# Block 2 computed with tokens on partitions one batch earlier, in a fused linear-attention and MLP kernel

## The chip, the cores and the metric

One core of one Trainium2 chip runs one program. The metric is the device time of one execution in microseconds (us), taken several times. The kernel before takes 304.78 us (median of 4 runs, 304.0 to 305.3, beside the changed kernel). TensorE is called PE, VectorE DVE, ScalarE ACT, GpSimd POOL and SyncE SP, as the profile does.

## The reference

Eight batches of eight heads with 576 tokens of 64 channels go through a linear attention with a norm. The 4608 x 512 result goes through two matrix products with a leaky rectifier between them.

```
kv  = einsum('bhsd,bhse->bhde', k, v)                   # 64 x 64 per head
out = einsum('bhsd,bhde->bhse', q, kv)
rms = sqrt(mean(out * out, -1) + 1e-6)
x   = (out / rms * g_norm) -> (4608, 512)               # 8 heads x 64 side by side
h   = x @ w_in                                          # 512 x 2048
g   = maximum(h, 0) + alpha * minimum(h, 0)
y   = g @ w_out                                         # 2048 x 512, float32
```

## The kernel before

The 4608 tokens are worked in nine windows of 512. In each, 16 groups of the hidden dimension pass through `m1` (four matmuls `h_ps`, then ACT `m_sb` and DVE `gt`), and `y_mm` multiplies the `gt` of the window before by `w_out`. Beside this stream, PE prepares the attention of the coming windows ("block w"), in one of two ways:

- *Channels on partitions* (batches below `NB_PE`): PE transposes q (`qt_ps`), multiplies (`ot_ps`), and sums squares with another matmul (`ssq_ps`); ACT and DVE make the norm.
- *Tokens on partitions* (batches from `NB_PE` on): one DMA transposes q (`qtm`). PE multiplies one tile of 128 tokens at a time (`otm_ps`), ACT, DVE and POOL make the norm along the free axis, and small DMA transposes bring the tile back into `xm`. PE does less here, since it transposes nothing and sums no squares.

```
NB_PE = 3
def load(b, nm, h0=0, h1=H):             # two DMAs, issued on GpSimd
    nc.gpsimd.dma_start(...); nc.gpsimd.dma_start(...)
def regroup_batch(b):                    # copies into the matmul layout
    for nm in ("k", "q"): regroup(b, nm, eng=nc.gpsimd)
...
def transpose_q(b):                      # issued on SyncE
    qtms[b] = attn_p.tile([P, NT * NPAIR, P], FP16, name="qtm")
    nc.sync.dma_start_transpose(out=qtms[b][:], in_=...bufs[b % NBUF]["q"]...)
...
# after the y matmuls of window 0 (about 52 us):
regroup_batch(2)
steps = window_steps(2)                  # block 2, channels on partitions
for g in range(NF):
    if g == 3:
        load_batch(3)
        regroup_batch(3)
    m1_group(1, g)
    ...                                  # one step of block 2, a y matmul, another step
    if g == NF - 4: nc.sync.dma_start(out=g_all[:], in_=g_norm[:].partition_broadcast(P))
    if g == NF - 3: transpose_q(3)
```

The opening is a chain without that stream: batch 0 is loaded in halves and goes through q transposes, kv, `ot`, `ssq` and norms. `keep_warm(n)` puts n matmuls on constant data between them, to keep PE busy.

## Time and profile before

| | before |
|---|---|
| median of 4 runs | 304.78 us |
| span of the profiled run (305.35 us) | 303.6 us |
| PE busy | 285.6 us (94%) |
| PE waits in block 2 (about 54 to 100 us) | 3.2 us |
| stretch at half clock | 22.4 to 29.2 us |
| steady stream of window 0 starts, ends | 23.83, 38.12 us |
| first group of window 1 starts | 54.43 us |

PE is nearly full, so one reads where it is not, and where its clock is halved. The prediction shows those lines. One more view is the timeline of POOL (columns: start, length, engine, line, operation, output and input, count, and in brackets the idle time before it with what ended that).

```profile
50.21 2.32 POOL L106 COPY qsb<-qst 128x2560 f16<-128x2560 f16 x1 [0.63 <-DMA qst<-in_q_dram]
52.47 0.68 POOL L96 DMA_DIRECT2D kst<-in_k_dram  x1
```

POOL regroups q of batch 2 and issues the loads of batch 3 directly after it. The issue stands behind the regroup on the same engine: in this order the loads are not issued before the data of batch 2 has come in and been copied.

### The profile page before, as it was taken

To read this page: it belongs to the slowest core of one execution; us is meant where nothing else is said; L and a number is where in the kernel's file an instruction comes from. 1 tells how busy PE (TensorE), PEld (TensorE's weight loads), DVE (VectorE), ACT (ScalarE), POOL (GpSimd) and SP (SyncE) were. 2 spreads that over 40 slices of the span, in tenths; PEclk is the share of its full clock that TensorE was granted. 3 is DMA by queue.
4 is the path that set the end of the run, shared out by engine and by line. 5 is a ranking of instruction groups with operands and counts; after the bars stand their busy time and mean duration, and the time that the engine had idled before them with its cause. 6 is when DMAs were issued, how large, how long until landed. Compare 5 with 4: busy or idle time off the path is not lost.

```text
span 303.6 us, 4204 instructions
## 1 busy us (share of the span) xinstructions
PE 285.6 (94%) x1526; PEld 136.6 (45%) x1526; DVE 163.1 (54%) x249; ACT 156.5 (52%) x298; POOL 96.8 (32%) x105
## 2 busy tenths in 40 slices
PE   5769999988999899999999999999999999999993
PEld 2423454453554455445544544455444444444441
DVE  4545853557665548544964585459546844344200
ACT  1364617749586338434844574458437544443320
POOL 9923306730018504660566056404101300000000
PEclk9995999999999999999999999999999999999999
DMA  7999999993118983995289839954311411112233
GB/s 95 189 206 200 203 203 163 147 195 89 35 35 96 193 189 28 147 213 136 56 122 214 148 69 149 185 119 70 79 35 37 95 35 35 37 40 55 45 71 69
DMA packets 61156, 34.33 MB, mean 113 GB/s; under 512 B 27840, under 2 KB 56528, under 8 KB 61136
## 3 DMA queue, kind: packets, MB, share of 16 engines
q0 software_dynamic: 29664, 18.35, 43.7%
q1 hardware_dynamic: 31472, 15.71, 24.5%
q8 instruction: 12, 0.20, 0.3%
q14 instruction: 8, 0.07, 0.1%
HBM read 36.74 MB, written 9.44 MB: 152 GB/s over the span
## 4 chain that ended last, share of the span: by engine, by line
PE 83%; ACT 4%; POOL 4%; DVE 3%; issue 2%; DMA 2%; POOLq 0%; ACTq 0%; DVEq 0%
PE h_ps L421 38%; PE y_ps L443 35%; PE kv_ps L231 3%; DMA qst<-in_q_dram 2%; PE otm_ps L339 2%; ACT m_sb L428 2%; ACT rstd L274 1%; POOL rg L363 1%; DVE gt L430 1%; PE qt_ps L210 1%; PE ssq_ps L272 1%; PE yc L443 1%; PE yb L443 1%; PE ya L443 1%; POOL qst L96 1%
## 5 line engine op out<-in xcount | busy, mean ns | idle before, releaser
L430 DVE SCALAR_TENSOR_TENSOR gt<-m_sb,beta_sb,h_ps 128x512 f16<-128x512 f32 x144 | 106.7, 744 | 81.9 <-ACT m_sb L428 81.1
L443 PE MATMUL y_ps<-w_out_sb,gt 128*128 128x512 f16 x528 | 134.8, 379 | 0.0
L428 ACT ACTIVATE m_sb<-h_ps 128x512 f32<-128x512 f32 x144 | 85.8, 597 | 92.4 <-PE h_ps L421 92.3
L421 PE MATMUL h_ps<-xm,w_in_sb 128*128 128x512 f16 x384 | 98.5, 379 | 0.0
L421 PEld LDWEIGHTS <-w_in_sb 128*128 128x128 f16 x576 | 55.7, 99 | 68.7 <-issue 10.0
L443 PEld LDWEIGHTS <-gt 128*128 128x128 f16 x576 | 55.9, 98 | 65.9 <-issue 2.2
L363 POOL TENSOR_TENSOR rg<-ss,g_all 128x512 f32<-128x512 f32 (+1 forms) x25 | 26.1, 1045 | 93.0 <-ACT ss L361 93.0
L421 PE MATMUL h_ps<-xt,w_in_sb 128*128 128x512 f16 x192 | 50.4, 397 | 3.4 <-DVE gt L430 1.9
L450 ACT COPY y_sb<-y_ps 128x512 f32<-128x512 f32 x33 | 19.2, 583 | 17.5 <-PE y_ps L443 17.4
L351 DVE TENSOR_REDUCE ss<-sqm_sb 128x8 f32<-128x512 f32 (+1 forms) x25 | 17.1, 683 | 8.3 <-ACT sqm_sb L345 8.2
L106 POOL COPY ksb<-kst 128x2560 f16<-128x2560 f16 x6 | 13.9, 2318 | 20.9 <-DMA kst<-in_k_dram 20.9
L372 DVE TENSOR_TENSOR xrow<-otm_ps,rg 128x512 f16<-128x512 f32 (+1 forms) x25 | 17.0, 681 | 6.4 <-POOL rg L363 6.4
L345 ACT ACTIVATE sqm_sb<-otm_ps 128x512 f32<-128x512 f32 (+1 forms) x25 | 14.8, 593 | 6.9 <-PE otm_ps L339 6.9
L106 POOL COPY qsb<-qst 128x2560 f16<-128x2560 f16 x6 | 13.9, 2323 | 12.0 <-DMA qst<-in_q_dram 12.0
L283 DVE SCALAR_TENSOR_TENSOR xt<-ot_ps,g2col,rstd 128x512 f16<-128x512 f32 x12 | 8.9, 749 | 12.0 <-ACT rstd L277 12.0
L262 ACT ACTIVATE sq_sb<-ot_ps 128x512 f16<-128x512 f32 x12 | 6.9, 589 | 15.7 <-PE ot_ps L256 15.7
L231 PE MATMUL kv_ps<-vst,ksb 128*128 128x128 f16 x160 | 10.4, 219 | 1.9 <-DVE qt_sb L219 1.3
L231 PEld LDWEIGHTS <-ksb 128*128 128x128 f16 x160 | 9.5, 98 | 5.5 <-DVE ksb L106 2.4
L274 ACT ACTIVATE rstd<-ssq_ps,eps_t 128x512 f32<-128x512 f32 x12 | 8.2, 684 | 4.5 <-PE ssq_ps L272 4.5
L339 PEld LDWEIGHTS <-qtm 128*128 128x128 f16 x100 | 7.7, 98 | 5.9
L339 PE MATMUL otm_ps<-kv_sb,qtm 128*128 128x128 f16 x100 | 9.7, 219 | 0.0
L195 PE MATMUL warm_ps<-warm,mask 128*128 128x512 f16 x15 | 6.0, 555 | 3.1 <-DVE eps_t L138 3.1
(56 smaller groups left out, 135.0 us busy)
## 6 DMA issues: line engine op xcount, KB each, us to landing
out_dram<-y_sb SPq DMA_DIRECT2D x72, 128.0 KB, 2.4
kst<-in_k_dram POOLq DMA_DIRECT2D x7, 320.0 KB, 5.4
qst<-in_q_dram POOLq DMA_DIRECT2D x7, 320.0 KB, 8.3
vst<-in_v_dram POOLq DMA_DIRECT2D x7, 320.0 KB, 10.8
w_in_sb<-in_moe_w_in_dram POOLq DMA_DIRECT2D x4, 512.0 KB, 10.1
w_out_sb<-in_moe_w_out_dram POOLq DMA_DIRECT2D x4, 512.0 KB, 16.0
kst<-in_k_dram POOLq DMA_DIRECT2D x7, 256.0 KB, 7.1
qst<-in_q_dram POOLq DMA_DIRECT2D x7, 256.0 KB, 9.7
```

Source lines behind the costliest of these rows:

```text
L106: (eng or nc.vector).tensor_copy(out=bufs[b % NBUF][nm][:, :, h0:h1, :].rearrange("p t h d -> p h t d"), in_=stages[b % NBUF][nm][:, h0:h1],)
L231: nc.tensor.matmul(out=kv_ps[:, j - j0, :], lhsT=ks(t), rhs=vs(t), start=(t == 0), stop=(t == NT - 1),)
L339: nc.tensor.matmul(out=ot_ps[:, 2 * j : 2 * j + 2, :], lhsT=qtms[b][:, t * NPAIR + j, :], rhs=kvs[b, j], start=True, stop=True,)
L345: nc.scalar.activation(out=sq[0:n], in_=ot_ps[0:n], func=AF.Square)
L351: nc.vector.tensor_reduce(out=ss[0:n], in_=sq[0:n], op=ALU.add, axis=mybir.AxisListType.X,)
L363: nc.gpsimd.tensor_tensor(out=rg[0:n], in0=ss[0:n].unsqueeze(2).to_broadcast([n, H, D]), in1=g_all[0:n].unsqueeze(1).to_broadcast([n, H, D ...
L372: nc.vector.tensor_mul(out=x[0:n], in0=ot_ps[0:n], in1=rg[0:n])
L421: nc.tensor.matmul(out=h_ps[:], lhsT=w_in_blk(c, g), rhs=xt_of(w, c), start=(c == 0), stop=(c == NC - 1),)
L428: nc.scalar.activation(out=m_sb[:], in_=h_ps[:], func=AF.Relu, scale=-1.0)
L430: nc.vector.scalar_tensor_tensor(out=gt[:], in0=m_sb[:], scalar=beta_sb[:, g : g + 1], in1=h_ps[:], op0=ALU.mult, op1=ALU.add,)
L443: nc.tensor.matmul(out=y[:], lhsT=gts[w, g][:, a * P : (a + 1) * P], rhs=w_out_blk(g), start=(g == 0), stop=(g == NF - 1),)
L450: nc.scalar.copy(out=y_sb[:], in_=y[:])
```

## The change

It computes block 2 with tokens on partitions too (`NB_PE` 2), since that takes less PE time. The q of batch 2 is regrouped on DVE (it comes first now) and transposed by DMA during window 0. The opening gets more keep-warm matmuls and other buffers, so that its clock does not dip. The norm weights `g_all`, wanted earlier now, are spread over the partitions by a matmul instead of a late DMA. The loads of batch 3 stand, in the source, before window 1, and k of batch 2 is regrouped on DVE there; batch 3 is regrouped later in window 1 than before (group 9 instead of 3).

```diff
-    NB_PE = 3
+    NB_PE = 2
 ...
-        for nm in ("k", "q", "v"):        # load_batch; regroup_batch likewise
+        for nm in ("q", "k", "v"):
 ...                                       # opening (cut: the other keep_warm lines)
-    keep_warm(3)
+    keep_warm(4)
     step_kv(0, 0, 2)
+    keep_warm(2)
 ...
+    diag = const_p.tile([P, D], FP32, name="diag")
+    nc.vector.tensor_scalar(
+        out=diag[0:D], in0=ident[0:D, 0:D], scalar1=g2col[0:D], scalar2=None, op0=ALU.mult,
+    )
+    g_ps = ps_y.tile([P, D], FP32, name="g_ps", tag="y")
+    nc.tensor.matmul(out=g_ps[:], lhsT=ones32[0:D], rhs=diag[0:D], start=True, stop=True)
+    nc.vector.tensor_copy(out=g_all[:], in_=g_ps[:])
 ...
-    step_ot(0, 2)
+    step_ot(0, 2, (ps_o, "o2"))
 ...                                       # in the y matmuls of window 0
+        if g == 9:
+            regroup(2, "q")                # on DVE
+            transpose_q(2)
+        if g == 13:
+            load_batch(3)
+            regroup(2, "k")                # on DVE
 ...
-    regroup_batch(2)
-    steps = window_steps(2)                # (cut: the whole loop of window 1 as above)
-    for w in range(2, NW):
+    for w in range(1, NW):                 # window 1 joins the common loop
```

More of the change, by code (lines that the diff above doesn't have):

```diff
@@ L111, in load_batch @@
     def load_batch(b):
-        for nm in ("k", "q", "v"):
+        for nm in ("q", "k", "v"):
             load(b, nm)
     def regroup_batch(b):
-        for nm in ("k", "q"):
+        for nm in ("q", "k"):
             regroup(b, nm, eng=nc.gpsimd)
@@ L134 @@
     nc.vector.tensor_copy(out=mask16[:], in_=mask32[:])
+    ones32 = const_p.tile([P, P], FP32, name="ones32")
+    nc.vector.memset(ones32[:], 1.0)
     warm16 = const_p.tile([P, W], FP16, name="warm16")
@@ L148 @@
     nc.sync.dma_start(out=alpha_row[:], in_=moe_alpha[:].rearrange("(g p) -> g p", p=P))
-    g_all = const_p.tile([P, D], FP32, name="g_all")
     WQ = 4
@@ L189, with keep_warm @@
         load_w_out(i)
-    def keep_warm(n):
-        ps = ps_s.tile([P, W], FP32, name="warm_ps", tag="s")
+    def keep_warm(n, pool=(ps_s, "s")):
+        ps = pool[0].tile([P, W], FP32, name="warm_ps", tag=pool[1])
         for i in range(n):
@@ L267, in step_ssq, with ssq_mm @@
         norm(w, j)
-    def ssq_mm(w, j):
+    def ssq_mm(w, j, pool=(ps_o, "o2")):
         ot_ps, sq = ots.pop((w, j))
-        ssq_ps = ps_o.tile([P, W], FP32, name="ssq_ps", tag="o2")
+        ssq_ps = pool[0].tile([P, W], FP32, name="ssq_ps", tag=pool[1])
         nc.tensor.matmul(out=ssq_ps[:], lhsT=mask16[:], rhs=sq[:], start=True, stop=True)
@@ L483 @@
     )
+    diag = const_p.tile([P, D], FP32, name="diag")
[3 more added lines that the diff above has]
+    g_ps = ps_y.tile([P, D], FP32, name="g_ps", tag="y")
+    nc.tensor.matmul(
+        out=g_ps[:], lhsT=ones32[0:D], rhs=diag[0:D], start=True, stop=True,
+    )
+    g_all = const_p.tile([P, D], FP32, name="g_all")
+    nc.vector.tensor_copy(out=g_all[:], in_=g_ps[:])
     regroup(0, "k", HH, H)
     ssq_mm(0, 0)
+    keep_warm(3)
     ssq_mm(0, 1)
+    norm(0, 0)
+    keep_warm(3)
     step_kv(0, 2, 4)
-    norm(0, 0)
     norm(0, 1)
-    step_ot(0, 2)
+    step_ot(0, 2, (ps_o, "o2"))
     step_ot(0, 3, (ps_y, "y"))
@@ L493 @@
     first = [ps_h.tile([P, W], FP32, name="h_ps", tag="h") for g in range(3)]
-    for g in range(3):
+    m1_mm(first[0], 0, 0, (0, 1))
+    ssq_mm(0, 2, (ps_s, "s"))
+    for g in (1, 2):
         m1_mm(first[g], 0, g, (0, 1))
-    step_ssq(0, 2)
-    keep_warm(2)
-    step_ssq(0, 3)
+    ssq_mm(0, 3, (ps_o, "o0"))
+    keep_warm(6, (ps_o, "o1"))
+    norm(0, 2)
+    norm(0, 3)
     for g in range(3):
         m1_mm(first[g], 0, g, (2,))
+    keep_warm(2, (ps_o, "o1"))
     for g in range(3):
@@ L524 @@
                 steps.pop(0)()
+        if g == 9:
[4 more added lines that the diff above has]
+            regroup(2, "k")
     for a in range(AHEAD):
         y_out(ys[a], 0, a)
-    regroup_batch(2)
-    steps = window_steps(2)
-    n = len(steps)
-    y = ps_y.tile([P, W], FP32, name="y_ps", tag="y")
-    for g in range(NF):
-        if g == 3:
-            load_batch(3)
-            regroup_batch(3)
-        m1_group(1, g)
-        if g > 3 and steps:
-            steps.pop(0)()
-        y_mm(y, 0, AHEAD, g)
-        if g > 3 and steps:
-            steps.pop(0)()
-        if g == NF - 4:
-            nc.sync.dma_start(out=g_all[:], in_=g_norm[:].partition_broadcast(P))
-        if g == NF - 3:
-            transpose_q(3)
-    y_out(y, 0, AHEAD)
     LOAD_G = 6
-    for w in range(2, NW):
+    for w in range(1, NW):
         steps = phase_steps(w + 1)
         for g in range(NF):
-            if g == LOAD_G and w + 2 < B:
+            if g == LOAD_G and 3 < w + 2 < B:
                 load_batch(w + 2)
             a, part = divmod(g, TPW)
-            if part == 0:
-                pool, tag = ((ps_y, "y"), (ps_s, "s"))[a % 2]
-                y = pool.tile([P, W], FP32, name="y_ps", tag=tag)
+            parts = range(part * TPW, (part + 1) * TPW)
+            if w == 1:
+                a, parts = AHEAD, [g]
             begin, mid, end = steps.pop(0) if steps else ([], [], [])
@@ L567 @@
                 f()
-            for gg in range(part * TPW, (part + 1) * TPW):
+            if parts[0] == 0:
+                pool, tag = ((ps_y, "y"), (ps_s, "s"))[a % 2 if w > 1 else 0]
+                y = pool.tile([P, W], FP32, name="y_ps", tag=tag)
+            for gg in parts:
                 y_mm(y, w - 1, a, gg)
-            if part == TPW - 1:
+            if parts[-1] == NF - 1:
                 y_out(y, w - 1, a)
```

## The prediction

> **What bounds the kernel now.** I read the page first, then the windows, the PE timeline and the DMA views. On the page, TensorE is busy in almost every slice, and the chain that ended last runs mostly through its matmuls:
>
> ```profile
> PE   5769999988999899999999999999999999999993
> PEclk9995999999999999999999999999999999999999
> DMA  7999999993118983995289839954311411112233
> ...
> PE 83%; ACT 4%; POOL 4%; DVE 3%; issue 2%; DMA 2%; POOLq 0%; ACTq 0%; DVEq 0%
> ```
>
> From about 75 us on there is little to win: 512-column matmuls start every 0.216 us (four `h_ps` pieces of the chain last 0.86 us) and the stores at the end remain. Time can come only from the opening, from block 2 (52 to 99 us), and from fewer matmuls. The PEclk row has a dip in the fourth slice, with PE rows under 9 before it. The windows show why (columns: stretch, length, PE, PEld, DVE, ACT, POOL busy, granted clock, DMA share, GB/s):
>
> ```profile
> 16.00:19.00 3.00, 2.69 (x11) 0.99 (x11) 0.88 (x2) 1.52 (x3) 0.76 (x1) 1.00 1.24 205
> 19.00:22.40 3.40, 1.59 (x6) 0.57 (x6) 1.50 (x2) 2.09 (x4) 0.94 (x2) 1.00 1.25 207
> 22.40:25.80 3.40, 2.65 (x7) 0.84 (x6) 2.06 (x3) 1.64 (x4) 1.19 (x2) 0.50 1.33 200
> 25.80:29.20 3.40, 3.40 (x9) 1.18 (x8) 1.49 (x2) 1.18 (x3) 1.49 (x2) 0.50 1.41 201
> 29.20:32.60 3.40, 3.40 (x17) 1.56 (x16) 2.36 (x4) 2.33 (x4) 1.38 (x2) 1.00 1.28 202
> ```
>
> A stretch with PE 47% busy is followed by two at clock 0.50: 9 matmuls in 3.4 us instead of 17. The DMA queue, too, is full from the start (about 200 GB/s) until 51 us. PE's idle time in block 2, from its timeline:
>
> ```profile
> 61.45 1.28 PE L231 MATMUL kv_ps<-vst,ksb 128*128 128x128 f16 x20 [1.34 <-DVE qt_sb L219]
> ...
> 71.15 0.38 PE L272 MATMUL ssq_ps<-sq_sb,mask 128*128 128x512 f16 x1 [0.55 <-ACT sq_sb L262]
> ...
> 99.42 1.02 PE L421 MATMUL h_ps<-xt,w_in_sb 128*128 128x512 f16 x4 [0.87 <-DVE gt L430]
> ```
>
> With two smaller ones (0.18, 0.25) that is 3.2 us. The last is GpSimd's: six load issues (92.8 to 96.9) stood before a norm product.
>
> **What the Trainium skill says.** "TensorE: Matmul & The Clock Gate", Part 1: the clock is gated to half when PE was not busy enough in a free-running window of 3413 ns, and freed after a busy one. The trace agrees: half clock from 22.4 to 29.2, two such windows. "DMA: Bandwidth & Descriptors", section "SWDGE vs HWDGE vs iDMA": loads issued from GpSimd and transfers issued from SyncE feed different queues of the same 16 engines, which take turns between them. The trace agrees. In 103 to 105 us, with both waiting, nearly as many packets of one as of the other passed (columns: packets, MB, share of 16 engines):
>
> ```profile
> q0 software_dynamic: 448, 0.28, 93.6%
> q1 hardware_dynamic: 409, 0.10, 38.4%
> ```
>
> Same page, "Latency and other measured facts": a DMA transpose reaches 261 GB/s. Alone it does here: 271 GB/s in 108 to 110 us.
>
> **The change, part by part.**
>
> *Opening.* Keep-warm matmuls go from 15 to 30, and two norms and two buffers move. (a) The clock: the slow window gets eight more matmuls (6 + 2, some 1.7 us at 0.216), so it goes from 47% to near 90% busy, and the clock should hold. From 23.83, when the steady stream starts, to 29.20 it ran at half: 5.37 / 2 = **2.7 us** won. (b) The cost: `g_ps` stands before the first `ssq` on PE and waits for beta and then the diagonal on DVE. Beta starts at 13.19 and takes 0.17, the diagonal about as long, and the fp32 matmul as long as `alpha_ps` (0.23). The first `ssq` moves from 12.79 to about 14.0. Against this, `ot` 2 no longer waits for the norm at 16.27 (its bank is another). Working the ACT chain through with the timeline's durations (Ln 0.69, Exp 0.63, square 0.58, norm 0.75), the steady stream starts at about 24.1, so **0.3 us** is lost. Net **-2.4**. The weights keep ahead: the last `w_in` lands at 24.7, `w_out` at 33.9, 39.1, 41.6 and 44.5 against needs of 35.7, 41.4, 45 and 48.7.
>
> *Block 2 on PE.* Removed: 20 transposes x 0.056, four `ot` (0.22 each), four `ssq` (0.22), the old tail of 4 x 0.083 and 2 x 0.163: 3.5 us. Added: five tiles x 4 x 0.056, a tail of 4 x 0.056 and one `ssq`: 1.55 us. Net **-1.95**.
>
> *Waits of block 2.* The wait for `qt_sb` has no counterpart, and the three norm products now stand ahead of the regroups and loads: **-3.2**.
>
> *g by a matmul.* The broadcast DMA (6.7 us to landing) is gone; it was hidden before. **0** besides (b).
>
> *New wait 1: kv of batch 2.* It was at 61.45, and moves to just after the first group of window 1: y starts at 35.7 instead of 38.1, so that group starts at about 52.0 and ends at 52.9. v of batch 2 lands at 53.1, k's regroup ends at about 53.3: **+0.5**.
>
> *New wait 2: the transposed q of batch 2.* q lands at 47.1; the regroup on DVE follows a norm and ends at about 48.7. Then comes a DMA transpose of 655 KB in 2560 packets of 256 B. Before, such transposes ran on an empty queue. The DMA view of 92 to 108 us has one, with its time from issue to landing in us:
>
> ```profile
> qtm<-qsb SPq DMA_TRANSPOSE x1, 4.5
> ```
>
> The small transposes of `xm` (91 to 101 us), at most 512 packets each:
>
> ```profile
> DMA to landing us min/median/max: 4.0/6.3/8.0
> ```
>
> 8.0 is one of 512 under load: some 4 us until its first packet, then about 200 packets per us. At 48.7 the queue is now not empty: before, batch 3's loads were issued at 52.5, because GpSimd's own regroup of batch 2 held them. Nothing on GpSimd holds them now; each waits only for the load eight before it (w_out's third, landed at 41.6, for the first), wherever the source puts the call. So 3072 packets of batch 3 pass together with the transpose. My estimate: 48.7 + 4 + 2560 / 215 + 0.6 = 65.2. The first tile wants it on PE at 52.0 + three groups of 1.08 + kv 1.1 + wait 0.5 + tail 0.4, about 57.3. **+8**. An idle PE also loses its clock: one or two windows at half, of which I count **+1.5**.
>
> Sum: -2.4 - 1.95 - 3.2 + 0.5 + 8 + 1.5 = +2.5, which is 307.
>
> **The rivals.**
> *A: the transpose comes in time.* For it: I found no transpose of this size under load, and the share of turns is read from small ones; q is loaded first and regrouped on DVE, which shows a design for just this. Then another engine binds window 1 for a while: one y matmul per group makes a group 1.08 us long on PE, plus 0.22 for a tile, while DVE has gt, the reduction and xrow (0.74 + 0.68 + 0.68, some 0.2 less back to back). Three tiles cost about 1.5 us. Sum: -7.55 + 0.5 + 1.5 = -5.5, **299**.
> *B: the clock dips again* because the windows lie elsewhere in other runs: +2.7 on either.
> *C: a middle course*: the engines serve pairs faster (280 per us, as the separate rates of 370 and 1130 would allow), the landing is 62, the wait 4.5 us and the clock costs less: **303 to 304**.
> Against the main line speaks only that its size is carried from 512 packets to 2560; for it, that every issue and landing up to 48 us follows from the same queue as before.
>
> **Range and chances.** I weigh the main line (307) at a little over half, A (299) at a third, and C between: the point is 304.5, and 299 to 309 should hold it 8 times in 10. Two per cent are 298.5 and 310.7. Faster needs A with less than 1.5 us of tile waits: 0.13. Slower needs the full wait with two slow windows and more: 0.05. Within: 0.82.
>
> **What would show each step.** Clock 1.0 from 9 us to at least 57; the steady stream starting at about 24 and y at 35.7. Keep-warm count 30. kv of batch 2 starting at 53.3 after a wait for `vst` or `ksb`. PE's `otm_ps` waiting for the DMA of `qtm`, with that DMA 13 to 17 us from issue to landing and the loads of batch 3 issued before 51 us; then half clock. No PE idle before the last groups of window 2. The prediction is wrong if that DMA lands in under 9 us, or if the opening's dip stays.

## The result, and the profile after

The changed kernel takes 308.78 us (median of 4 runs, 308.4 to 309.8). The ratio to the kernel before is 1.014, with a 95% interval of 1.011 to 1.017: within 2%, but clearly slower. Ratios here are the mean time of one kernel's fast runs over that of the other's fast runs of the same rounds, so they are not quite the ratio of the medians. The profiled spans are 306.7 us after and 303.6 us before.

The page of the kernel after, with the rows of busy tenths and the chain that ended last:

```profile
PE   5698999549999999999999999999999999999993
PEclk9999999959999999999999999999999999999998
DMA  7999999992524993897169919943311411112233
...
PE 84%; DMA 7%; DVE 2%; POOL 2%; ACT 2%; issue 1%; POOLq 0%; ACTq 0%
```

The dip of the clock in the fourth slice is gone, and a new one stands in the ninth, where PE (slices 8 and 9) is at 5 and 4. The chain now holds 7% of DMA where it held 2%. The windows of the kernel after (columns as in the prediction) give both places:

```profile
19.00:22.40 3.40, 3.36 (x17) 1.40 (x16) 0.77 (x2) 3.29 (x6) 0.69 (x1) 1.00 1.25 207
22.40:25.80 3.40, 2.36 (x11) 0.94 (x10) 2.30 (x4) 1.57 (x3) 1.14 (x2) 1.00 1.30 205
...
58.50:62.00 3.50, 0.00 (x0) 0.00 (x0) 1.40 (x2) 0.68 (x2) 0.00 (x0) 1.00 1.33 186
62.00:65.50 3.50, 0.00 (x0) 0.00 (x0) 0.00 (x0) 0.00 (x0) 0.00 (x0) 0.52 1.30 212
65.50:69.00 3.50, 3.26 (x14) 1.74 (x15) 0.96 (x2) 1.47 (x4) 0.00 (x0) 0.51 0.57 187
69.00:72.00 3.00, 3.00 (x18) 1.49 (x17) 2.84 (x5) 2.57 (x7) 2.06 (x2) 1.00 0.00 0
```

In the opening PE does 17 matmuls where it did 6, and the clock stays at 1.00. From 58.5 to 65.5 PE does nothing at all. The clock falls in the middle of that, and comes back at 69. PE's timeline names what it waited for:

```profile
14.43 0.43 PE L492 MATMUL g_ps<-diag,ones 64*128 64x64 f32 x2 [0.98 <-DVE diag L488]
...
25.03 2.32 PE L422 MATMUL h_ps<-xt,w_in_sb 128*128 128x512 f16 x10 [1.03 <-DVE gt L431]
...
54.23 1.29 PE L232 MATMUL kv_ps<-vst,ksb 128*128 128x128 f16 x20 [0.36 <-DVE ksb L106]
...
65.74 0.61 PE L340 MATMUL otm_ps<-kv_sb,qtm 128*128 128x128 f16 x4 [7.41 <-DMA qtm<-qsb]
```

The last line is the loss: the first tile of batch 2 waits 7.41 us for its transposed q. The chain of waits says when that DMA was issued and how long it took (columns: start, length, what):

```profile
49.60 16.09 DMA qtm<-qsb
```

The prediction showed a transfer of the same size at 4.5 us (that of batch 4, issued at 106.5, with the last loads gone by 108). The DMA view of 54 to 64 us shows the company (columns: packets, MB, share of 16 engines), and POOL's timeline where it comes from:

```profile
q0 software_dynamic: 2279, 1.27, 87.9%
q1 hardware_dynamic: 2281, 0.58, 43.7%
```

```profile
42.45 0.68 POOL L96 DMA_DIRECT2D qst<-in_q_dram  x1 [2.12 <-DVE qt_sb L220]
...
51.16 0.69 POOL L96 DMA_DIRECT2D vst<-in_v_dram  x1 [2.78 <-PE ya L444]
```

The loads of batch 3 are issued from 42.45 us on; before, the first was issued at 52.47. No regroup on POOL holds them any more. In ten microseconds the engines passed 2279 packets of loads and 2281 of the transpose, 228 per us each: as many of one as of the other.

The balance of the two profiled runs, by PE's timeline, in us (after minus before; the fewer matmuls are the prediction's count):

| term | difference |
|---|---|
| first group of window 1 starts at 52.83 instead of 54.43 | -1.60 |
| wait for `qtm` | +7.41 |
| wait for k of batch 2 (`ksb`) | +0.36 |
| PE's work at half clock, 65.74 to 68.94, half of it lost | +1.60 |
| a wait for `gt` at 75 us that was not there | +0.59 |
| waits of block 2 that went away | -3.19 |
| fewer matmuls | -1.95 |
| sum | +3.22 |
| spans: 306.7 - 303.6 | +3.1 |

So the change does what it was meant to do, and loses more to one transfer. The measured times differ by about 4.2 us (0.0139 x 304.8), more than the profiles: the profiled run of before took 305.35 us, a little over the four timed beside it.

### The profile page after: what moved, and what is told of

It reads as the page before. It is cut to its first block, busy times and chain, and to the rows that moved or that the text cites. A ratio compares the mean times of both kernels' runs of the same rounds, so it can differ in the third digit from the quotient of the medians.

```text
span 306.7 us, 4237 instructions
## 1 busy us (share of the span) xinstructions
PE 284.5 (93%) x1530; PEld 136.7 (45%) x1530; DVE 166.9 (54%) x255; ACT 153.2 (50%) x298; POOL 97.3 (32%) x108
## 4 chain that ended last, share of the span: by engine, by line
PE 84%; DMA 7%; DVE 2%; POOL 2%; ACT 2%; issue 1%; POOLq 0%; ACTq 0%
PE h_ps L422 38%; PE y_ps L444 37%; DMA qtm<-qsb 5%; PE kv_ps L232 3%; PE otm_ps L340 2%; DMA vst<-in_v_dram 2%; PE warm_ps L196 1%; ACT m_sb L429 1%; PE ssq_ps L273 1%; DVE gt L431 1%; PE ya L444 1%; PE yc L444 1%; PE yb L444 1%; PE qt_ps L211 1%; PE ot_ps L257 1%
## 5 line engine op out<-in xcount | busy, mean ns | idle before, releaser
L422 PE MATMUL h_ps<-xm,w_in_sb 128*128 128x512 f16 x448 | 115.0, 379 | 0.0
L364 POOL TENSOR_TENSOR rg<-ss,g_all 128x512 f32<-128x512 f32 (+1 forms) x30 | 31.3, 1042 | 99.5 <-ACT ss L362 98.7
L422 PE MATMUL h_ps<-xt,w_in_sb 128*128 128x512 f16 x128 | 32.2, 388 | 1.9 <-DVE gt L431 1.9
L352 DVE TENSOR_REDUCE ss<-sqm_sb 128x8 f32<-128x512 f32 (+1 forms) x30 | 20.5, 683 | 16.1 <-ACT sqm_sb L346 16.0
L346 ACT ACTIVATE sqm_sb<-otm_ps 128x512 f32<-128x512 f32 (+1 forms) x30 | 17.8, 592 | 15.8 <-PE otm_ps L340 15.7
L373 DVE TENSOR_TENSOR xrow<-otm_ps,rg 128x512 f16<-128x512 f32 (+1 forms) x30 | 20.5, 682 | 3.6 <-POOL rg L364 3.6
L340 PE MATMUL otm_ps<-kv_sb,qtm 128*128 128x128 f16 x120 | 12.1, 225 | 7.4 <-DMA qtm<-qsb 7.4
L196 PE MATMUL warm_ps<-warm,mask 128*128 128x512 f16 x30 | 9.7, 461 | 3.8 <-DVE eps_t L140 3.3
L284 DVE SCALAR_TENSOR_TENSOR xt<-ot_ps,g2col,rstd 128x512 f16<-128x512 f32 x8 | 6.0, 750 | 9.2 <-ACT rstd L278 9.2
L359 ACT ACTIVATE ss<-ss,eps_t 128x8 f32<-128x8 f32 (+1 forms) x30 | 9.0, 300 | 2.9 <-DVE ss L352 2.9
```

Of the source, the lines that this page charges most:

```text
L340: nc.tensor.matmul(out=ot_ps[:, 2 * j : 2 * j + 2, :], lhsT=qtms[b][:, t * NPAIR + j, :], rhs=kvs[b, j], start=True, stop=True,)
L346: nc.scalar.activation(out=sq[0:n], in_=ot_ps[0:n], func=AF.Square)
L352: nc.vector.tensor_reduce(out=ss[0:n], in_=sq[0:n], op=ALU.add, axis=mybir.AxisListType.X,)
L364: nc.gpsimd.tensor_tensor(out=rg[0:n], in0=ss[0:n].unsqueeze(2).to_broadcast([n, H, D]), in1=g_all[0:n].unsqueeze(1).to_broadcast([n, H, D ...
L373: nc.vector.tensor_mul(out=x[0:n], in0=ot_ps[0:n], in1=rg[0:n])
L422: nc.tensor.matmul(out=h_ps[:], lhsT=w_in_blk(c, g), rhs=xt_of(w, c), start=(c == 0), stop=(c == NC - 1),)
```

## The experiments

The theory: the transpose is late because the loads of batch 3 share the DMA engines with it, packet for packet. The main rival: a transpose of this size, issued there, is late anyway, and only a smaller or an earlier one would help. A second question is what the opening gained and what the `g_ps` matmul cost in it. Each call ran on one chip with its own runs of the kernel before. Three calls took eleven runs; their medians of before were 304.23, 305.24 and 305.34 us.

**e1_hold3: the transpose alone.** A copy of four columns of `qtm` on POOL, ahead of the loads of batch 3, holds them until the transpose has landed. Nothing else is changed.

```diff
         if g == 13:
+            held = const_p.tile([P, 4], FP16, name="held")
+            nc.gpsimd.tensor_copy(out=held[:], in_=qtms[2][:, 0, 0:4])
             load_batch(3)
```

> The changed kernel, but GpSimd issues batch 3's loads only after the transposed q of batch 2 has landed (it first copies four of its columns). Theory T (the transpose took 16 us because its packets take turns with those of batch 3's loads): the transpose lands before 58 us, under 9 us after its issue, PE waits for it less than 0.5 us instead of 7.4, the clock stays at 1.0, and some 1 us of tile waits on DVE appears instead of the slow clock: about 300.5 us, 8 less than the changed kernel. Rival U (a transpose of 2560 packets takes this long at that place anyway, or batch 2's own loads hold it up): it still takes over 12 us and the time stays above 306. Possible new wait: kv of batch 3 at the start of window 2, since its v lands some 7 us later.

Measured: 301.12 us (300.91 to 301.43), ratio 0.990 (0.986 to 0.995). Answers of the trace on `qtm`, of POOL's timeline, and of the list of PE's waits (total, times, longest):

```profile
DMA to landing us min/median/max: 7.4/7.4/7.4
```

```profile
56.89 0.19 POOL L549 COPY held<-qtm 128x4 f16<-128x4 f16 x1 [16.80 <-DMA qtm<-qsb]
57.38 0.68 POOL L96 DMA_DIRECT2D qst<-in_q_dram  x1 [0.30 <-issue]
```

```profile
PE otm_ps L340 <- DVE xm L314: 1.2, 1, 1.2
```

The transfer takes 7.4 us instead of 16.1, PE does not wait for it, and the clock stays at 1.00 from the opening on. Nothing about the transpose itself was changed, so the rival falls: the late landing is the company. By the ratios the kernel gains 0.0235 x 304.5 = 7.2 us over the kernel after (the run of before at 308.0 is slow and left out of the ratios). The trace accounts for it: 7.41 + 1.60 won, 1.20 lost to a new wait for a PSUM bank that the tile shares with the norm of the tail, about 0.5 to one more wait for `gt` and 0.24 to a longer one for kv: 7.1.

**e2_split5 and e3_split2: leave the loads, cut the transpose.** The transpose is one DMA of five tiles; PE needs only the first to go on. e2 issues one DMA per tile, e3 one of three tiles and one of two. The loads of batch 3 stay early.

```diff
-        nc.sync.dma_start_transpose(out=qtms[b][:], ...)
+        for t0, t1 in ([(t, t + 1) for t in range(NT)] if b == 2 else [(0, NT)]):   # e3: [(0, 3), (3, NT)]
+            nc.sync.dma_start_transpose(
+                out=qtms[b][:, t0 * NPAIR : t1 * NPAIR, :], in_=...["q"][:, t0:t1]...)
```

> The changed kernel, with batch 2's q transposed in five DMAs, one tile (512 packets) each, loads as in the changed kernel. T: the first lands about 57 us (4 us to its first packet, 512 packets at about 225 per us, 0.6 to land), the others 2.3 us apart, so that PE waits under 1 us in total for the first three and the time is about 301 us. U (the transpose is slow as such): the sum over five issues is no quicker, the first tile still waits over 5 us, 306 or more.

> The same in two DMAs, the first with the three tiles that window 2 needs (1536 packets), the second with two. T: the first lands at about 49.6 + 3.6 + 1536 / 230 + 0.6 = 60.5 us, so PE waits some 2.2 us (7.4 in the changed kernel, with 2560 packets); the clock holds; about 302.5 us. A wait that does not follow the number of packets would be against T.

e2 measured 300.91 us (300.34 to 301.23), ratio 0.990 (0.984 to 0.996). Its five parts landed at 56.2, 58.6, 61.1, 63.4 and 65.5 us: one every 2.3 us, each ahead of its tile. So the last q still comes at 65.5, as in the kernel after, and costs nothing. The times to landing, and the first tile in PE's timeline:

```profile
DMA to landing us min/median/max: 7.3/9.5/10.9
```

```profile
58.88 0.38 PE L342 MATMUL otm_ps<-kv_sb,qtm 128*128 128x128 f16 x4 [1.20 <-DVE xm L314]
```

What is left there is the wait for the PSUM bank, as in e1. e3 had one run: 303.81 us, its state unknown. Its first part landed at 60.84 against an expected 60.5, and PE waited less than half as long. The expectation had the clock hold and the time at 302.5; both were missed: the clock was slow from 61.64 to 65.06, one window instead of two. Its waits of PE:

```profile
PE otm_ps L342 <- DMA qtm<-qsb: 3.1, 1, 3.1
```

With 2560, 1536 and 512 packets ahead of the first tile, PE waits 7.4, 3.1 and 0 us for the DMA. The expectation for e3 was worked out from 228 packets per us, so the rate carries. (The wait was 3.1 us and not the expected 2.2, as the part landed 0.3 later and PE was there 0.5 earlier than in the kernel after.)

**e4_warm30: the wait stays, the clock does not fall.** Thirty keep-warm matmuls fill the wait.

```diff
+            if a == [(2, 0)]:
+                end.insert(0, lambda: keep_warm(30))
```

> The changed kernel, with 30 keep-warm matmuls (6.5 us) put on PE ahead of the first tile of batch 2, where it only waits. The transpose lands as before at about 65.7 us; the clock stays at 1.0 where it was 0.5 from 62.1 to 68.9 us. If the slow clock is worth what I counted (3.2 us of PE work at half rate, 1.6 us), the time is about 307.2; if DVE's tile work binds there anyway, 308 to 309, as the changed kernel.

Measured: 307.31 us (306.89 to 307.67), ratio 1.011 (1.006 to 1.016). The windows of e4:

```profile
62.00:65.50 3.50, 2.41 (x15) 1.06 (x14) 0.00 (x0) 0.06 (x1) 0.00 (x0) 1.00 1.28 240
65.50:69.00 3.50, 3.50 (x24) 1.85 (x23) 2.58 (x4) 2.91 (x8) 1.04 (x1) 1.00 0.45 138
```

PE passes 24 matmuls in the second stretch instead of 14, at full clock. The time is 1.5 us under the kernel after by medians, 1.0 us by ratios; the two intervals overlap, and part of the gain is not the clock: in e4's profile the transpose also landed 0.7 us earlier (64.97, issued at 48.68), and one more wait for `gt` cost 0.5. With 1.6 for the clock the difference of the profiled spans, 1.8, closes to 0.1, so that price is supported and not pinned down. The greater part of the loss is the wait itself.

**e5_opening_no_g and e6_opening_g: the opening alone.** Both are the kernel before with the refilled opening. e5 keeps the late DMA for `g_all`, e6 takes the `g_ps` matmul in the place where the change has it.

```diff
-    keep_warm(3)                 # e5: the opening's lines of the change, without diag and g_ps
+    keep_warm(4)
     step_kv(0, 0, 2)
+    keep_warm(2)
 ...
+    g_ps = ...                   # e6 alone, before ssq_mm(0, 0); the late DMA of g_all goes
```

> The kernel before with the refilled opening alone (15 more keep-warm matmuls, the moved norms and banks), g by its DMA as before. In the first call's seven runs of the kernel before, the three at clock 1.0 took about 303.0 us and the two at 0.986 to 0.989 about 305.6: the dip is not there in every run. If my step holds (the filling costs 0.3 us, the g matmul the rest), every run has clock 1.0 and takes about 303.3 us, the steady stream starting near 24.1 us. Rival: the filling itself, not g, costs the 1.2 us that the changed kernel's stream started later (25.0 against 23.8): about 304.1.

> The same with g spread by the matmul at its place in the changed kernel. All of the opening's change, nothing of block 2's. Stream at 25.0, clock 1.0: about 304.1 us in every run, which is 1.2 above an undipped run of the kernel before and 1.4 below a dipped one. If g costs nothing, as my prediction had it beyond its 0.3, equal to the run without g.

e5 measured 302.67 us (302.31 to 305.45), ratio 0.992 (0.987 to 0.997). e6 measured 304.42 us (303.33 to 306.92), ratio 0.997 (0.992 to 1.003). They ran on the same chip. The waits of PE, in e5 (first line) and in e6:

```profile
PE kv_ps L231 <- DMA vst<-in_v_dram: 3.6, 1, 3.6
```

```profile
PE g_ps L491 <- DVE diag L487: 1.0, 1, 1.0
```

The matmul is wanted late and placed early: it waits about 1 us for DVE's diagonal, on the chain of the opening. From the first kv matmul to the steady stream it is 13.98 us before, 14.57 in e6 and 14.62 in the kernel after; with the matmul behind the chain (e9, e11) it is 13.55 and 13.37. So refilling shortens the chain by about 0.5 us, and the matmul adds 1.0 to 1.2. (The old opening takes the same 13.99 in e10b, whose clock held.)

e5 also shows that refilling does not keep the clock up in every run. Four of its six runs took 302.3 to 302.7 us at a mean clock of 0.996 or more; the profiled one, 305.45, waited 3.6 us for a late v and lost its clock afterwards. Nor is every slow run a dip: two runs of e6, at mean clocks of 1.000 and 0.996, took 305.67 and 305.01, for a reason that no kept trace shows. And the dip of the kernel before is not in each of its runs. In the first call its runs at a mean granted clock of 1.0 took 302.9 to 303.1 us (three runs), at 0.994 304.2, at 0.986 to 0.989 305.4 to 305.7, and at 0.978 308.0. One slow window is worth 0.0056 of the mean clock (an estimate: half of 3.4 us, as two windows took 6.8 us in the trace, over 303 us), so these are about none, one, two and four. The profile of before, with its two windows, is a middling draw: of 29 runs of before, 3 were at 1.0, 11 at 0.994 and 15 at 0.989 or less, with a mean of 0.989, about two windows. Undipped runs of e5 are only about 0.5 us under undipped runs of before (which sat on another chip); its average gain of 2.5 us (0.0082 x 305.2) would then be mostly rarer dips.

**e9_best: the parts together.** e2's five transposes, `g_ps` behind the first three groups of the stream (`diag` stays where it was, early), and another PSUM bank for the first tile.

```diff
-    n_tile = [0]
+    n_tile = [1]
 ...                              # g_ps and g_all moved to here
+    g_ps = ...
     for g in range(3, NF):
         m1_group(0, g)
```

> The changed kernel with batch 2's transpose in five, the g matmul moved behind the first three groups of the first product (out of the opening's chain), and the first tile of batch 2 in another PSUM bank than the tail, whose norm it waited for (1.2 us in the run with five transposes). About 0.9 from g and up to 1.2 from the bank off 300.9: 299.0 us. If DVE's tile work binds behind the bank's wait, only 299.8.

Measured: 300.47 us (299.75 to 301.7), ratio 0.984 (0.979 to 0.988). The expectation of 299.0 was missed. The wait for the bank is gone, but PE arrives sooner at kv of batch 2, and v is not there. PE's timeline of e9:

```profile
54.15 1.28 PE L232 MATMUL kv_ps<-vst,ksb 128*128 128x128 f16 x20 [1.48 <-DMA vst<-in_v_dram]
```

**e10_best_old_opening and e10b_old_opening: e9 with the opening of before.** The first was faulty: its `diag` stood behind three `gt` on DVE, and PE waited 2.75 us for it (305.63 us, ratio 1.001); it tells nothing about the opening. The second has `diag` early.

> The same with the opening of the kernel before. If the refilled opening costs 0.3 us and saves 2.7 in runs with a dip: 298.7 us in runs at clock 1.0 and about 301.3 in dipped runs, so that its runs spread and the refilled one's do not. If the refilling costs the 1.2 us itself: 298 in undipped runs.

> The last run mended: there the diagonal for g stood behind three gt's on DVE, so PE waited 2.75 us for it, a fault of the edit. Now it stands early, as in the refilled version. Old opening, transposes in five, other bank. Undipped runs: about 300.4 (as the refilled version, whose opening is no longer); runs with the clock slow for one, two or three windows of 3.4 us: some 1.3, 2.7 and 4 us more. If the refilling is what keeps the clock up, most of these runs are dipped, the median is 302 or more and it is slower than the refilled version by 1.5 to 3.

Measured: 301.42 us (299.73 to 302.66), ratio 0.987 (0.983 to 0.991), with mean clocks from 0.983 to 0.999. Its two runs at 0.998 and more took 299.7 and 300.0 us, no longer than e9's; the other four, at 0.983 to 0.994, took 301.4 to 302.7. Against e9's 0.984 that is about 1 us for the refilled opening. The intervals overlap and the chips differ, so its worth beside the new block 2 stays open.

**e11_kv_later: a later kv.** e9, but kv of batch 2 stands two groups later in window 1 and the tiles one group later.

```diff
+            steps.append(([], [], []))                       # after the tail's steps
-            steps[0][1].append(lambda: step_kv(w))
+            steps[2 if w == NB_PE else 0][1].append(lambda: step_kv(w))
```

> The refilled version with transposes in five, the early g out of the way and the other bank, in which PE then waited 1.48 us for v of batch 2 (landed at 54.0) at kv, with kv moved from group 0 to group 2 of window 1 and the tiles one group later. kv comes at about 55.0 us, after v: no wait there. If the load of v is the floor there: 1.4 off, 299.0 us. If DVE's tile work takes it back: 300.4.

Measured: 298.19 us (297.47 to 298.42, 5 runs), ratio 0.977 (0.973 to 0.980). This version beats both kernels, and is 0.8 us below its expectation of 299.0. The largest waits of PE that are left, beside those of the opening (of the 1.4, 0.7 stands at the start of the stream and 0.45 in window 1):

```profile
PE h_ps L425 <- DVE gt L434: 1.4, 3, 0.7
PE otm_ps L342 <- DMA qtm<-qsb: 0.6, 1, 0.6
```

**e12_kv_later_spaced: room after each tile.** e11 with an empty group after each tile of batch 2, against the waits for `gt`.

> The same with a group without a tile after each tile of window 1, so that DVE has two groups (2.4 us of PE) for the reduction, xrow and two gt's (2.9 us at full length, some 2.5 back to back). The three waits for gt of the refilled version (0.55, 0.61, 0.59) shrink to under 0.6 in all: 297.8 us, over 2 per cent faster than the kernel before. Possible new wait: the last tile's transpose into xm for window 2.

Measured: 298.65 us (298.19 to 299.24), ratio 0.978 (0.975 to 0.982): no gain, where 297.8 was expected. In window 1 it has three waits for `gt` (0.18, 0.60 and 0.58 us), against 0.55, 0.61 and 0.59 in e9 and a single one of 0.45 in e11.

All runs beside their own runs of before:

| run | what | median us | ratio |
|---|---|---|---|
| after | the change | 308.78 | 1.014 |
| e4 | + keep-warm in the wait | 307.31 | 1.011 |
| e3 | transpose in two parts | 303.81 (one run) | - |
| e1 | loads held | 301.12 | 0.990 |
| e2 | transpose in five parts | 300.91 | 0.990 |
| e6 | before + opening + `g_ps` | 304.42 | 0.997 |
| e5 | before + opening | 302.67 | 0.992 |
| e10b | e9 with the old opening | 301.42 | 0.987 |
| e9 | e2 + late `g_ps` + bank | 300.47 | 0.984 |
| e12 | e11 + empty groups | 298.65 | 0.978 |
| e11 | e9 + later kv | 298.19 | 0.977 |

## Why the prediction was right or wrong

The measured 308.78 lies inside the range of 299 to 309, near its upper edge, and "within 2%" was the likeliest class. But the forecast of 304.5 said that next to nothing would change, and the change costs a clear 1.4%. Point by point:

- **The clock in the opening**: right. The steady stream of window 0 takes 11.65 us instead of 14.29 in the two profiled runs, 2.64 us against a predicted 2.7. The one trace could not tell how often the dip comes; that its two windows are about the mean of the 29 runs was luck.
- **The cost in the opening**: mis-sized. "0.3 us is lost" took `g_ps` as a matmul that fits in. The stream started at 25.03, not at 24.1, and PE waited 0.98 us for the diagonal. "g by a matmul: 0 besides (b)" has the same fault. The net of the opening was -1.44 in the profiles at the start of y, not -2.4, and about -0.8 in e6's runs (ratio 0.997, with an interval that reaches 1.003). In the profiles, part of the difference is the first kv, which could start only 0.6 us later in that run, since v came later.
- **Block 2 on PE and its waits**, -1.95 and -3.2: right as far as the balance shows, which closes with them to 0.1 us.
- **New wait 1**, +0.5: right, 0.36.
- **New wait 2**, +8: right. Issue 49.60 (48.7 predicted), landing 65.69 (65.2), wait 7.41. The loads were issued from 42.45 as argued, and e1 showed that they are the cause.
- **The clock after it**, +1.5: right by the trace, 1.6, in two windows; e4 kept the clock up and won 1.0 to 1.5.
- **The rivals**: A needed the transpose in time, and C a faster sharing; the 228 packets per us of each queue exclude both. B, a dip in the opening in spite of the filling, did not occur in the profile of the kernel after, but did in the profiled run of e5, behind a late v.

The step that failed is the weighing: "I weigh the main line (307) at a little over half, A (299) at a third, and C between". The main line was right in its mechanism and nearly right in each large term of block 2. A, in which the transpose comes in time, got a third because no transpose of this size had been seen under load and because the order of loads "shows a design for just this", that is, from trust in intent; in the run the transpose landed 7.41 us after PE wanted it. The lines that spoke against it, 448 packets of one queue beside 409 of the other, were measured. The weighted mean of two futures that differ by 8 us lies where only C could have put it. The second fault is the size of the opening: with -1.44 instead of -2.4 the main line would have said 308.

## What to carry to other kernels

A step on one engine can be the gate for what stands behind it on that engine: when the loads no longer stood behind the regroup on GpSimd, they went out 10 us earlier (42.45 instead of 52.47), into the transfer that the next step needed. (By the order on GpSimd, moving the regroup or moving the loads in the source would each have done it; no run tries one alone.) Before moving such a step, ask what it was holding back, and hold or cut the transfers that meet: here, cutting the transfer to what its first reader needs took its wait away with the others still in flight (e2), and putting a reader a little later helped too (e11). When a sum rests on measured rates and its rival on an assumed intention, forecast the sum; and before valuing the removal of a dip, look in several runs for whether it is there.

## What the Trainium skill lacked or had wrong

- "DMA: Bandwidth & Descriptors", "SWDGE vs HWDGE vs iDMA", says that the engines take turns between the queues, and so it was: in ten microseconds 2279 and 2281 packets passed. It lacks the consequence: a DMA transpose of 655 KB took 16.1 us beside loads, 7.4 us with those of batch 3 held back, and 4.5 us where the last loads were gone 1.5 us after its issue.
- The same page, "Latency and other measured facts", gives 261 GB/s for a DMA transpose with a non-contiguous middle dimension, and does not say what else may be in flight. Alone it reached 271 GB/s here; beside loads 0.58 MB passed in 10 us on its queue, 58 GB/s.
- The same page, "Queues, rings and completion order", has turns of whole packets of about 9 to 17 descriptors. The profile's own packets, 256 B each for the transpose, passed in equal numbers; the page does not say how the two counts are related.
- No page has a start-up figure for a transfer in a full queue: the first packet of this transpose was seen at about 53.7 us, 4 us after its issue at 49.60; in e1, with the loads of batch 3 held, 2.1 us after it (51.46 after 49.4).
- "TensorE: Matmul & The Clock Gate", Part 1, gives windows of 3413 ns, and the half clock came in multiples of it (6.8 us in before and in after, 3.4 us in e3). It lacks the threshold. Cut from each clock change into windows of 3.413 us, the 13 traces show it between close limits: full-clock windows with PE busy 0, 21, 22, 43 and 46% (the last in the kernel before, 18.96 to 22.38) were followed by half clock (as were windows at the very end, when the work stops), and none with 51% or more was (busy by this profile, whose matmul ends are modelled). So where the windows fall decides: e10b, with the old opening, had 67 and 59% there and kept its clock. The page says that the ramp varies between runs; here the same kernel took 302.9 us without a dip and 308.0 us with a mean clock of 0.978.
